# Attention feeding a two-layer MLP: one batch of tokens at a time, with attention steps woven between matmul groups in a written order

## The chip, the cores and the metric

The kernel runs on one core of a Trainium2 chip. A core has five engines with a queue each: TensorE (PE, matmuls out of SBUF into PSUM), VectorE (DVE), ScalarE (ACT), GpSimd (POOL, which here mostly issues DMAs) and SyncE (SP, which issues the output DMAs). Each queue runs its instructions in its own order, and instructions of different engines wait for one another by semaphores. PSUM has 8 banks of 512 fp32 values in each of 128 partitions. The metric is the device time of one execution in microseconds (us); lower is better.

## What is computed

Linear attention without softmax, an RMS norm per head, and a two-layer MLP with a PReLU, from the reference:

```python
batch, n_heads, seq, head_dim = (8, 8, 576, 64)
kv = np.einsum('bhsd,bhse->bhde', k, v)
out = np.einsum('bhsd,bhde->bhse', q, kv)
rms = np.sqrt(np.mean(out * out, axis=-1, keepdims=True) + 1e-06)
attn_out = (out / rms * g_norm)
x = attn_out.transpose(0, 2, 1, 3).reshape(B * S, H * D)      # 4608 x 512
h = x @ w_in                                                  # 512 x 2048
g = np.maximum(h, 0.0) + alpha * np.minimum(h, 0.0)
return (g @ w_out)                                            # 4608 x 512, fp32
```

## The kernel before

Data is fp32 in HBM; POOL's DMAs cast it to fp16 while loading. Heads are taken in pairs, so that one pair (2 x 64 rows) fills the 128 partitions: 4 pairs a batch, 32 in all.

Attention of a pair is split into four functions. `attn_fea` (L131 on) transposes q of the pair in five matmuls against an identity (L136, L145) and copies the result to SBUF on ACT. `attn_feb` makes k-transposed times v for each of the two heads in five matmuls of 64 columns (L163), copies it, and multiplies it with q-transposed for each head by itself, in a part of 512 and a part of 64 columns (L179, L183); DVE copies the result `ot` to SBUF. `attn_be1` squares it on DVE, sums the squares over the 64 rows of each head by a matmul with a two-column selector `esel` (L198, L201), and takes exp(-0.5 ln(mean + eps)) on two partitions on ACT (L205 to L214). `attn_be2` spreads the two rows back over 128 partitions by a matmul with `eselT` (L224, L227), and DVE multiplies `ot`, the gain and that into `xt` (L230, L235), which is kept for all 4608 tokens. `astep` (L288 on) runs these four functions for four different pairs in one call.

The MLP runs over 12 windows of 384 tokens. `moe_m1` makes the 16 blocks of 128 hidden features of a window, each from 4 chunks of the contraction (L247); ACT casts each block from PSUM to fp16 (L255) and DVE applies the PReLU as max(alpha h, h) (L257). `moe_m2` (L264 on) makes three tiles of 128 tokens, each from 16 matmuls of 512 columns (L269), copied by ACT (L277) and stored by SP.

The order of the work around it: for each window first as many `astep` calls as its tokens need, then the whole of `moe_m1` (64 matmuls in a row), two `astep` calls, the whole of `moe_m2` of the window before (48 in a row), two `astep` calls. All PSUM tiles share one pool of 8 banks. POOL loads q, k and v of batches 0 and 1, then w_in, w_out, then further batches, each batch as 3 tensors of 5 row chunks (L111). The identity is made behind the first of these loads.

Of the kernel before, what the change touches and what calls it, by code (L numbers as in the profile page):

```python
# [10 lines left out]
FP16 = mybir.dt.float16  # L12


@with_exitstack
def kernel(
# [11 lines left out]
    nc = tc.nc  # L28
# [7 lines left out]
    S_CH = [128, 128, 128, 128, 64]  # L36
    NT = len(S_CH)
    S_OFF = [0, 128, 256, 384, 512]
    NWIN = 384
    N_WINDOWS = N_TOK // NWIN  # L40
    NF = D_FF // P
    NC = D_MODEL // P
    assert NC == NPAIR
# [4 lines left out]
    xt_p = ctx.enter_context(tc.tile_pool(name="xt", bufs=1))  # L48
    qkv_p = ctx.enter_context(tc.tile_pool(name="qkv", bufs=3))
    attn_p = ctx.enter_context(tc.tile_pool(name="attn", bufs=2))  # L50
    gt_p = ctx.enter_context(tc.tile_pool(name="gt", bufs=2))
    ysb_p = ctx.enter_context(tc.tile_pool(name="ysb", bufs=3))
    psum_p = ctx.enter_context(tc.tile_pool(name="psum", bufs=8, space=bass.MemoryType.PSUM))
# [13 lines left out]
    ident = const_p.tile([P, P], FP32, name="ident")  # L67
# [8 lines left out]
    esel32 = const_p.tile([P, 2], FP32, name="esel32")  # L76
    nc.vector.memset(esel32[:], 0.0)
    nc.vector.memset(esel32[0:64, 0:1], 1.0)
    nc.vector.memset(esel32[64:128, 1:2], 1.0)
    esel = const_p.tile([P, 2], FP16, name="esel")  # L80
    nc.vector.tensor_copy(out=esel[:], in_=esel32[:])
    eselT_ps = psum_p.tile([2, P], FP32, name="eselT_ps", tag="pb")
    nc.tensor.matmul(
        out=eselT_ps[:], lhsT=esel32[:], rhs=ident[:, :], is_transpose=True,
        start=True, stop=True,
    )
    eselT = const_p.tile([2, P], FP16, name="eselT")
    nc.scalar.copy(out=eselT[:], in_=eselT_ps[:])

    g2col = const_p.tile([P, 1], FP32, name="g2col")  # L90
# [3 lines left out]
    alpha_sb = const_p.tile([P, NF], FP32, name="alpha_sb")  # L94
    with nc.allow_non_contiguous_dma("tiny alpha load"):
        nc.sync.dma_start(
            out=alpha_sb[:], in_=moe_alpha[:].rearrange("(g p) -> p g", p=P)
        )

    xt_sb = [xt_p.tile([P, N_TOK], FP16, name=f"xt{j}") for j in range(NC)]  # L100

    def load_qkv(b):
        tiles = {}
        for nm, src in (("q", q), ("k", k), ("v", v)):
            t = qkv_p.tile([P, NT, H, D], FP16, name=f"{nm}sb", tag=f"{nm}sb")
            tiles[nm] = t
            eng = nc.gpsimd
            for ti in range(NT):
                ps = S_CH[ti]
                st = S_OFF[ti]  # L110
                eng.dma_start(  # L111
                    out=t[0:ps, ti, :, :],
                    in_=src[b, :, st : st + ps, :].rearrange("h s d -> s h d"),
                )
        return tiles

    qkv0 = load_qkv(0)
    qkv1 = load_qkv(1)

    w_in_sb = []  # L120
    for c in range(NC):
        t = w_p.tile([P, D_FF], FP16, name=f"w_in_sb{c}")
        nc.gpsimd.dma_start(out=t[:], in_=moe_w_in[c * P : (c + 1) * P, :])
        w_in_sb.append(t)
    w_out_sb = []
    for g in range(NF):
        t = w_p.tile([P, D_MODEL], FP16, name=f"w_out_sb{g}")
        nc.gpsimd.dma_start(out=t[:], in_=moe_w_out[g * P : (g + 1) * P, :])  # L128
        w_out_sb.append(t)

    def attn_fea(b, j, tiles):  # L131
        qs = tiles["q"]
        hs = slice(2 * j, 2 * j + 2)
        qt_a = psum_p.tile([P, 512], FP16, name="qt_a", tag="pb")
        for ti in range(4):
            nc.tensor.matmul(  # L136
                out=qt_a[:, ti * 128 : (ti + 1) * 128],
                lhsT=qs[0:128, ti, hs, :],
                rhs=ident16[:, :],
                is_transpose=True,  # L140
                start=(ti == 0),
                stop=(ti == 3),
            )
        qt_b = psum_p.tile([P, 64], FP16, name="qt_b", tag="pb")
        nc.tensor.matmul(  # L145
            out=qt_b[:, 0:64], lhsT=qs[0:64, 4, hs, :], rhs=ident16[0:64, 0:64],
            is_transpose=True, start=True, stop=True,
        )
        qt_sb = attn_p.tile([P, S], FP16, name="qt_sb", bufs=3)
        nc.scalar.copy(out=qt_sb[:, 0:512], in_=qt_a[:])  # L150
        nc.scalar.copy(out=qt_sb[:, 512:576], in_=qt_b[:])
        return (b, j, tiles, qt_sb)

    def attn_feb(st):
        b, j, tiles, qt_sb = st
        ks, vs = tiles["k"], tiles["v"]
        hA = slice(2 * j, 2 * j + 1)
        hB = slice(2 * j + 1, 2 * j + 2)
        kv4 = psum_p.tile([P, 64], FP32, name="kv4", tag="pb")
        for half, hsel in ((0, hA), (1, hB)):  # L160
            for ti in range(NT):
                ps = S_CH[ti]
                nc.tensor.matmul(  # L163
                    out=kv4[64 * half : 64 * half + 64, :],
                    lhsT=ks[0:ps, ti, hsel, :],
                    rhs=vs[0:ps, ti, hsel, :],
                    start=(ti == 0),
                    stop=(ti == NT - 1),
                    tile_position=(0, 64 * half),
                )  # L170
        kv_sb = attn_p.tile([P, 64], FP16, name="kv_sb")
        nc.scalar.copy(out=kv_sb[:], in_=kv4[:])  # L172

        ot_a = psum_p.tile([P, 512], FP32, name="ot_a", tag="pb")
        ot_b = psum_p.tile([P, 64], FP32, name="ot_b", tag="pb")
        for half in range(2):
            rs = slice(64 * half, 64 * half + 64)
            tp = (64 * half, 64 * half)
            nc.tensor.matmul(  # L179
                out=ot_a[rs, :], lhsT=kv_sb[rs, :], rhs=qt_sb[rs, 0:512],  # L180
                start=True, stop=True, tile_position=tp,
            )
            nc.tensor.matmul(  # L183
                out=ot_b[rs, :], lhsT=kv_sb[rs, :], rhs=qt_sb[rs, 512:576],
                start=True, stop=True, tile_position=tp,
            )
        ot_sb = attn_p.tile([P, S], FP32, name="ot_sb", bufs=5)
        nc.vector.tensor_copy(out=ot_sb[:, 0:512], in_=ot_a[:])  # L188
        nc.vector.tensor_copy(out=ot_sb[:, 512:576], in_=ot_b[:])
        return (b, j, ot_sb)  # L190

    def attn_be1(st):
        b, j, ot_sb = st
        sq_sb = attn_p.tile([P, S], FP16, name="sq_sb")
# [25 lines left out]
    def attn_be2(st):  # L220
# [17 lines left out]
            op0=mybir.AluOpType.mult, op1=mybir.AluOpType.mult,  # L238
        )

    def moe_m1(w):
        n0 = w * NWIN
        gts = []
        for g in range(NF):
# [116 lines left out]
```

## Time and profile before

| | us |
|---|---|
| median of 3 runs | 399.4 |
| lowest and highest | 399.25, 403.49 |
| profiled execution: span from first to last instruction | 400.0 |
| PE busy in it | 361.5 (90%) |
| DVE, ACT, POOL busy in it | 194.1, 186.4, 111.9 |

The lines of the profile stand in the prediction, each ahead of what is read from it. "PE" rows are matmuls, "PEld" rows are weight loads. In a timeline row the columns are the start and the length of a run of equal instructions, engine, source line, operation, tiles (out<-in), shape and count, and in brackets the idle time in front with what ended it. In a row of the grouped lines the two numbers behind the first bar are the busy time in us and the mean length of one in ns; behind the second bar stands the engine's idle time ahead of them.

### The profile page before, as it was taken

How to read it: one execution, taken by the hardware profiler on the slowest of the kernel's cores; microseconds unless marked ns; L12 is line 12 of the kernel's file. 1: busy time of each engine (PE TensorE's matmuls, PEld its weight loads, DVE VectorE, ACT ScalarE, POOL GpSimd, SP SyncE). 2: the span in 40 equal slices, each digit the busy share in tenths (PEclk: the TensorE clock that was granted, in tenths of full speed). 3: DMA queues.
4: the chain of work that ended last, by engine and by line, in shares of the span. 5: the costliest groups of instructions: out<-in, count | busy, mean ns of one | idle time of the engine just before them, and what ended most of it. 6: DMA issues, size and time to landing. Idle time of an engine off the chain costs nothing.

```text
span 400.0 us, 5448 instructions
## 1 busy us (share of the span) xinstructions
PE 361.5 (90%) x2081; PEld 182.0 (45%) x2081; DVE 194.1 (49%) x358; ACT 186.4 (47%) x422; POOL 111.9 (28%) x146
## 2 busy tenths in 40 slices
PE   2389967999999999999999999979999999999996
PEld 0144433453445446344544534444545455555542
DVE  0056744594178149507825841780735444453600
ACT  2056644573367257426736733661535353444511
POOL 9992799998044440800000000000000000000000
PEclk9999985596989889698999969898999999999999
DMA  9999999999394963950001002001001010101022
GB/s 85 142 143 206 195 143 141 140 145 140 90 59 28 120 87 25 96 78 26 2 26 54 0 2 79 2 0 47 34 26 55 26 54 26 53 10 70 2 79 79
DMA packets 122826, 28.15 MB, mean 70 GB/s; under 512 B 115632, under 2 KB 117680, under 8 KB 122800
## 3 DMA queue, kind: packets, MB, share of 16 engines
q0 software_dynamic: 115392, 18.36, 62.1%
q1 hardware_dynamic: 7408, 9.45, 6.7%
q8 instruction: 16, 0.26, 0.3%
q14 instruction: 10, 0.08, 0.1%
HBM read 36.71 MB, written 9.44 MB: 115 GB/s over the span
## 4 chain that ended last, share of the span: by engine, by line
PE 74%; POOL 9%; ACT 8%; DMA 6%; issue 1%; DVE 1%; POOLq 0%; ACTq 0%
PE y_ps L269 34%; PE h_ps L247 31%; DMA w_in_sb<-in_moe_w_in_dram 3%; POOL vsb L111 3%; PE ot_a L179 3%; POOL qsb L111 3%; PE ssq_a L198 2%; POOL ksb L111 2%; ACT qt_sb L150 2%; ACT rstd L214 2%; DMA qsb<-in_q_dram 2%; PE rb_a L224 2%; ACT lnv L205 2%; PE kv L163 1%; DMA vsb<-in_v_dram 1%; POOL w_out_sb L128 1%
## 5 line engine op out<-in xcount | busy, mean ns | idle before, releaser
L257 DVE SCALAR_TENSOR_TENSOR gt<-h,alpha_sb 128x384 f16<-128x384 f16 x192 | 117.2, 618 | 54.3 <-ACT h L255 49.4
L269 PE MATMUL y_ps<-w_out_sb,gt 128*128 128x512 f16 x576 | 136.2, 400 | 0.0
L247 PE MATMUL h_ps<-xt,w_in_sb 128*128 128x384 f16 x768 | 134.9, 339 | 0.0
L255 ACT CAST h<-h_ps 128x384 f16<-128x384 f32 x192 | 91.1, 478 | 38.4 <-PE h_ps L247 37.1
L247 PEld LDWEIGHTS <-w_in_sb 128*128 128x128 f16 x768 | 77.1, 101 | 57.1 <-issue 11.0
L269 PEld LDWEIGHTS <-gt 128*128 128x128 f16 x576 | 58.3, 102 | 75.9 <-issue 15.6
L188 DVE COPY ot_sb<-ot_a 128x512 f32<-128x512 f32 x32 | 22.1, 691 | 110.1 <-PE ot_b L183 110.1
L277 ACT COPY y_sb<-y_ps 128x512 f32<-128x512 f32 x36 | 21.1, 586 | 111.7 <-PE y_ps L269 111.7
L111 POOL DMA_DIRECT2D qsb<-in_q_dram x40 | 34.3, 936 | 23.2 <-PE qt_b L145 22.7
L111 POOL DMA_DIRECT2D ksb<-in_k_dram x40 | 34.3, 961 | 23.1 <-PE kv L163 23.1
L163 PE MATMUL kv<-vsb,ksb 128*64 128x64 f16 (+1 forms) x320 | 31.2, 218 | 8.8 <-DMA vsb<-in_v_dram 8.8
L205 ACT ACTIVATE lnv<-ssq_a,eps_t 2x512 f32<-2x512 f32 x32 | 21.7, 677 | 33.1 <-PE ssq_b L201 33.1
L111 POOL DMA_DIRECT2D vsb<-in_v_dram x40 | 34.6, 994 | 0.5 <-DMA qsb<-in_q_dram 0.4
L230 DVE SCALAR_TENSOR_TENSOR xt<-ot_sb,g2col,rb_a 128x512 f16<-128x512 f32 x32 | 23.8, 743 | 15.8 <-PE rb_b L227 15.8
L163 PEld LDWEIGHTS <-ksb 128*64 128x64 f16 (+1 forms) x320 | 22.2, 120 | 15.9 <-issue 10.0
L179 PE MATMUL ot_a<-qt_sb,kv_sb 64*64 64x512 f16 x64 | 16.4, 504 | 12.8 <-ACT kv_sb L172 12.8
L150 ACT COPY qt_sb<-qt_a 128x512 f16<-128x512 f16 x32 | 18.5, 577 | 12.6 <-PE qt_a L136 12.6
L195 DVE TENSOR_TENSOR sq_sb<-ot_sb 128x576 f16<-128x576 f32 x32 | 24.0, 751 | 0.1
L136 PE MATMUL qt_a<-ident,qsb 128*128 128x128 f16 x128 | 15.9, 250 | 8.0 <-DMA qsb<-in_q_dram 8.0
L214 ACT ACTIVATE rstd<-lnv 2x576 f16<-2x576 f32 x32 | 21.7, 679 | 0.4
L136 PEld LDWEIGHTS <-qsb 128*128 128x128 f16 x128 | 9.6, 108 | 17.9 <-DMA qsb<-in_q_dram 9.4
L198 PE MATMUL ssq_a<-sq_sb,esel 128*2 128x512 f16 x32 | 15.0, 469 | 1.7 <-DVE sq_sb L195 1.7
(35 smaller groups left out, 118.2 us busy)
## 6 DMA issues: line engine op xcount, KB each, us to landing
out_dram<-y_sb SPq DMA_DIRECT2D x36, 256.0 KB, 2.0
qsb<-in_q_dram POOLq DMA_DIRECT2D x32, 128.0 KB, 4.6
ksb<-in_k_dram POOLq DMA_DIRECT2D x32, 128.0 KB, 4.6
vsb<-in_v_dram POOLq DMA_DIRECT2D x32, 128.0 KB, 4.6
w_in_sb<-in_moe_w_in_dram POOLq DMA_DIRECT2D x4, 512.0 KB, 10.3
w_out_sb<-in_moe_w_out_dram POOLq DMA_DIRECT2D x16, 128.0 KB, 4.9
qsb<-in_q_dram POOLq DMA_DIRECT2D x8, 64.0 KB, 4.3
ksb<-in_k_dram POOLq DMA_DIRECT2D x8, 64.0 KB, 4.5
```

What stands on the lines that cost most here:

```text
L111: eng.dma_start(out=t[0:ps, ti, :, :], in_=src[b, :, st : st + ps, :].rearrange("h s d -> s h d"),)
L136: nc.tensor.matmul(out=qt_a[:, ti * 128 : (ti + 1) * 128], lhsT=qs[0:128, ti, hs, :], rhs=ident16[:, :], is_transpose=True, start=(ti == 0 ...
L150: nc.scalar.copy(out=qt_sb[:, 0:512], in_=qt_a[:])
L163: nc.tensor.matmul(out=kv4[64 * half : 64 * half + 64, :], lhsT=ks[0:ps, ti, hsel, :], rhs=vs[0:ps, ti, hsel, :], start=(ti == 0), stop=(t ...
L179: nc.tensor.matmul(out=ot_a[rs, :], lhsT=kv_sb[rs, :], rhs=qt_sb[rs, 0:512], start=True, stop=True, tile_position=tp,)
L195: nc.vector.tensor_mul(out=sq_sb[:], in0=ot_sb[:], in1=ot_sb[:])
L205: nc.scalar.activation(out=lnv[:, 0:512], in_=ssq_a[:], func=mybir.ActivationFunctionType.Ln, bias=eps_t[0:2, :], scale=inv_d,)
L214: nc.scalar.activation(out=rstd2[:], in_=lnv[:], func=mybir.ActivationFunctionType.Exp, bias=0.0, scale=-0.5,)
L247: nc.tensor.matmul(out=h_ps[:], lhsT=w_in_sb[c][:, g * P : (g + 1) * P], rhs=xt_sb[c][:, n0 : n0 + NWIN], start=(c == 0), stop=(c == NC - 1),)
L255: nc.scalar.copy(out=h16[:], in_=h_ps[:])
L257: nc.vector.scalar_tensor_tensor(out=gt[:], in0=h16[:], scalar=alpha_sb[:, g : g + 1], in1=h16[:], op0=mybir.AluOpType.mult, op1=mybir.Alu ...
L269: nc.tensor.matmul(out=y_ps[:], lhsT=gts[g][:, a * P : (a + 1) * P], rhs=w_out_sb[g][:], start=(g == 0), stop=(g == NF - 1),)
```

## The change

The kernel is rewritten around one batch (576 tokens) at a time:

- The tokens of a batch are two halves of 288 columns. Every PSUM tile of attention's `ot` and norm sum and of the first layer's block is two banks, one half in each, and one instruction of ACT or DVE takes both halves (576 values).
- A pair's k-transposed times v is made as one 128 x 128 product in five matmuls, and the blocks off the diagonal are set to zero by a multiplication with a mask on DVE. `ot` then takes two matmuls for both heads.
- The squares are summed by a matmul with the same mask in fp16 (128 x 128 blocks of ones), so that the sum stands on all 128 partitions at once. The selector, its transposition and the spreading matmuls are gone; Ln and Exp run on 128 partitions.
- The PReLU is h + (1 - alpha) relu(-h): a Relu on ACT out of PSUM, then one DVE instruction that reads PSUM too.
- PSUM is split by use: two tiles of two banks for the first layer, one bank for the second, one bank for q-transposed and kv (`ps_s`), one tile of two banks for `ot` and the norm sum (`ps_b`).
- The order of all engines is the order of the program text. A stream of steps (ot, t, ssq, kv of neighbouring pairs, 16 steps a batch) is taken one step at a time behind each of the 16 first-layer groups, with a share of the second-layer matmuls between them.
- Batch 0 is loaded in halves of 4 heads, ahead of the identity; w_in and w_out come in four pieces each, and w_in comes ahead of batch 1.

The diff, cut to its core (what is taken away stands whole in the listing above):

```diff
+    ps_h = ctx.enter_context(tc.tile_pool(name="psh", bufs=2, space=bass.MemoryType.PSUM))
+    ps_y = ctx.enter_context(tc.tile_pool(name="psy", bufs=1, space=bass.MemoryType.PSUM))
+    ps_s = ctx.enter_context(tc.tile_pool(name="pss", bufs=1, space=bass.MemoryType.PSUM))
+    ps_b = ctx.enter_context(tc.tile_pool(name="psb", bufs=1, space=bass.MemoryType.PSUM))
+    ctx.enter_context(tc.manual_schedule(engines={ENG.PE, ENG.Activation, ENG.DVE, ENG.Pool, ENG.SP}))
...
+    for j in range(0, NPAIR, 2):
+        for nm in ("k", "v", "q"):
+            load_heads(0, nm, 2 * j, 2 * j + 4)
...
+    load_w_in()
+    load_batch(1)
+    load_w_out()
+    load_batch(2)
...
+    def step_t(st):
...
+        st["qt"] = attn_p.tile([P, S], FP16, name="qt_sb")
+        nc.vector.tensor_copy(out=st["qt"][:], in_=qt_ps[:, 0:S])
+    def step_kv(st):
...
+        nc.vector.tensor_mul(out=st["kv"][:], in0=kv_ps[:], in1=mask32[:])
+    def step_ot(st):
+        ot_ps = ps_b.tile([P, 2, 512], FP32, name="ot_ps", tag="b")
+        for i in range(2):
+            nc.tensor.matmul(
+                out=ot_ps[:, i, 0:HS], lhsT=st["kv"][:], rhs=st["qt"][:, i * HS : (i + 1) * HS],
+                start=True, stop=True,
+            )
...
+        nc.scalar.activation(out=st["sq"][:], in_=ot_ps[:, :, 0:HS], func=AF.Square)
...
+        nc.vector.tensor_copy(out=st["ot"][:], in_=ot_ps[:, :, 0:HS])
+    def step_ssq(st):
...
+                out=ssq_ps[:, i, 0:HS], lhsT=mask16[:], rhs=st["sq"][:, i, :],
...
+            out=lnv[:], in_=ssq_ps[:, :, 0:HS], func=AF.Ln, bias=eps_t[:], scale=inv_d,
...
+        nc.scalar.activation(out=rstd[:], in_=lnv[:], func=AF.Exp, bias=0.0, scale=-0.5)
+        nc.vector.scalar_tensor_tensor(
+            out=xts[b, j][:],
+            in0=st["ot"][:], scalar=g2col[:], in1=rstd[:], op0=ALU.mult, op1=ALU.mult,
+        )
+    def step_stream():
+        for b in range(B):
+            st = [{"b": b, "j": j} for j in range(NPAIR)]
+            for j in range(NPAIR + 1):
+                if j > 0:
+                    yield step_ot, st[j - 1], False
+                if j < NPAIR:
+                    yield step_t, st[j], False
+                if j > 0:
+                    yield step_ssq, st[j - 1], j == NPAIR
+                if j < NPAIR:
+                    yield step_kv, st[j], False
...
+    def m1_group(b, g, big=False):
+        pool, tag = (ps_b, "b") if big else (ps_h, "h")
+        h_ps = pool.tile([P, 2, 512], FP32, name="h_ps", tag=tag)
+        for c in range(NC):
+            for i in range(2):
+                nc.tensor.matmul(
+                    out=h_ps[:, i, 0:HS], lhsT=w_in_blk(c, g), rhs=xts[b, c][:, i, :],
+                    start=(c == 0), stop=(c == NC - 1),
                 )
...
+        nc.scalar.activation(out=m_sb[:], in_=h_ps[:, :, 0:HS], func=AF.Relu, scale=-1.0)
...
+            in0=m_sb[:], scalar=beta_sb[:, g : g + 1], in1=h_ps[:, :, 0:HS],
...
+    class M2:
...
+        def run(self, n, limit):
+            while n > 0 and self.t < limit:
+                if self.g == 0:
+                    self.y = ps_y.tile([P, 512], FP32, name="y_ps", tag="y")
+                y_mm(self.y[:], self.t, self.g)
+                self.g += 1
+                n -= 1
+                if self.g == NF:
+                    y_out(self.y[:], self.t)
+                    self.t, self.g = self.t + 1, 0
...
+    attn_until(0)
     for g in range(NF):
+        m1_group(0, g, g % 3 == 2)
+    ya = ps_h.tile([P, 2, 512], FP32, name="ya", tag="h")
+    yb = ps_h.tile([P, 2, 512], FP32, name="yb", tag="h")
+    ys = [ya[:, 0, :], ya[:, 1, :], yb[:, 0, :], yb[:, 1, :]]
+    for g in range(NF):
+        for t in range(4):
+            y_mm(ys[t], t, g)
+        attn_step()
+    for t in range(4):
+        y_out(ys[t], t)
+    m2.t = 4
+    attn_until(1)
+    for b in range(1, B):
+        if b + 2 < B:
+            load_batch(b + 2)
+        limit = (b * S) // P
+        total = max(0, (limit - m2.t) * NF - m2.g)
+        done = 0
         for g in range(NF):
+            m1_group(b, g)
+            want = total * (g + 1) // NF
+            m2.run(want - done, limit)
+            done = want
+            attn_step()
...
+    m2.run(10**9, N_TOK // P)
```

By this text batch 1 has no second-layer matmuls between its groups (`limit` is 4, and those tiles are done), batches 2, 4 and 6 have 80 (5 behind each group), batches 3, 5 and 7 have 64 (4 behind each group), and the last 80 stand behind everything.

Three places show what moves. On POOL at the start, before (loads are q, k, v of batch 0; `ident` is the identity):

```order
masks.py:197 MEMSET ident 128x128
L111 DMA qsb<-in_q_dram 128x8x64
masks.py:199 ISA
masks.py:199 AFFINE_SELECT ident<-ident 128x128
L111 DMA qsb<-in_q_dram 128x8x64 x3
L111 DMA qsb<-in_q_dram 64x8x64
```

On POOL at the start, now:

```order
L89 DMA vsb_93<-in_v_dram 128x4x64 x4
L89 DMA vsb_93<-in_v_dram 64x4x64
L89 DMA qsb_95<-in_q_dram 128x4x64 x4
L89 DMA qsb_95<-in_q_dram 64x4x64
masks.py:197 MEMSET ident 128x128
masks.py:199 ISA
masks.py:199 AFFINE_SELECT ident<-ident 128x128
L133 DMA w_in_sb_159<-in_moe_w_in_dram 128x4x512
```

The identity, on which the transposes of q wait, moved from behind one load to behind all thirty of batch 0, which are half as large each.

On DVE in the attention of batch 0, before (`ot_sb` is the copy of `ot`, `sq_sb` the squares):

```order
L230 SCALAR_TENSOR_TENSOR xt_104<-ot_sb,g2col,rb_a 128x512 [waits DMAHW1_49,DMAHW0_49,PE_49]
L235 SCALAR_TENSOR_TENSOR xt_104<-ot_sb,g2col,rb_b 128x64 [waits PE_49]
L195 TENSOR_TENSOR sq_sb<-ot_sb 128x576 [waits DVE_49]
L188 COPY ot_sb<-ot_a 128x512 [waits PE_49]
L189 COPY ot_sb<-ot_b 128x64 [waits PE_49]
```

On DVE at the same place, now (`kv_sb` is the masked kv):

```order
L216 COPY ot_sb<-ot_ps 128x576 [waits Activation_49]
L189 COPY qt_sb<-qt_ps 128x576 [waits PE_49]
L233 SCALAR_TENSOR_TENSOR xt<-ot_sb,g2col,rstd 128x576 [waits DVE_49,Activation_49]
L204 TENSOR_TENSOR kv_sb<-kv_ps,mask_153 128x128 [waits PE_49]
L216 COPY ot_sb<-ot_ps 128x576 [waits Activation_49]
```

The copies of kv and of q-transposed came over from ACT, the squares went there, the copy of `ot` waits for ACT's Square, and the kv of a pair stands behind the `xt` of the pair before, which waits for ACT's Exp.

On PE where a second-layer tile ends and the next begins, before (weights `gt` are the hidden values of 128 tokens):

```order
L269 MATMUL y_ps<-w_out_sb_180,gt 128x512
L269 LDWEIGHTS gt
L269 MATMUL y_ps<-w_out_sb_182,gt 128x512
L269 LDWEIGHTS gt
L269 MATMUL y_ps<-w_out_sb_152,gt 128x512 [waits PE_49]
```

On PE at such a place now, inside the work of batch 2 (one of the four per batch that fall inside a run):

```order
L296 MATMUL y_ps<-w_out_sb_188,gt 128x512
L296 LDWEIGHTS gt
L296 MATMUL y_ps<-w_out_sb_182,gt 128x512 [waits Activation_49]
L296 LDWEIGHTS gt
L296 MATMUL y_ps<-w_out_sb_182,gt 128x512
L196 LDWEIGHTS ksb_91
L196 MATMUL kv_ps<-vsb_93,ksb_91 128x128 [waits DVE_49]
```

With one bank for the second layer, the first matmul of a tile waits for ACT's copy of the tile before; the attention step and the next first-layer group stand behind it on PE.

More of the change, by code (lines that the diff above doesn't have):

```diff
@@ L91 @@
-    nc.sync.dma_start(out=g2col[0:64, :], in_=g_norm[:].unsqueeze(1))
-    nc.sync.dma_start(out=g2col[64:128, :], in_=g_norm[:].unsqueeze(1))
[L94 to L97, printed above, removed]
-        )
[L100 to L113, printed above, removed]
-                )
-        return tiles
@@ L117 @@
[L117 to L125, printed above, removed]
-    for g in range(NF):
[L127 to L190, printed above, removed]
```

305 lines of the change are left out of this document (153 added, 152 removed).

## The prediction

> **What bounds the kernel now.** I read the page first: busy shares, the slices of time, and the shares of the chain that ended last.
>
> ```profile
> span 400.0 us, 5448 instructions
> PE 361.5 (90%) x2081; PEld 182.0 (45%) x2081; DVE 194.1 (49%) x358; ACT 186.4 (47%) x422; POOL 111.9 (28%) x146
> PEclk9999985596989889698999969898999999999999
> PE 74%; POOL 9%; ACT 8%; DMA 6%; issue 1%; DVE 1%; POOLq 0%; ACTq 0%
> ```
>
> TensorE (PE) is the bound, no other engine is half busy, and the granted clock dips until about 270 us. Next the chain in order of time, for where PE is not the bound and for the pure price of a matmul.
>
> ```profile
> 26.85 1.36 POOL w_in_sb L123 x3
> 28.21 13.20 DMA w_in_sb<-in_moe_w_in_dram
> ...
> 302.88 10.40 PE h_ps L247 x64
> 313.28 10.36 PE y_ps L269 x48
> ...
> 375.56 20.73 PE y_ps L269 x96
> 396.30 0.03 ACTq L277
> ...
> 396.36 0.58 ACT y_sb L277
> ```
>
> Until 41 us the chain is POOL issuing loads, then the w_in transfer. At the end PE runs without a gap: 10.40/64 = 162.5 ns for 384 columns, 10.36/48 = 215.8 ns for 512. Last PE's timeline, one attention burst of two pairs and what follows such bursts.
>
> ```profile
> 183.90 12.25 PE L247 MATMUL h_ps<-xt,w_in_sb 128*128 128x384 f16 x64
> 195.99 0.39 PE L136 MATMUL qt_a<-ident,qsb 128*128 128x128 f16 x4
> 196.31 0.20 PE L145 MATMUL qt_b<-ident,qsb 64*128 64x64 f16 x1
> 196.44 0.84 PE L163 MATMUL kv<-vsb,ksb 128*64 128x64 f16 x10
> 197.58 0.41 PE L179 MATMUL ot_a<-qt_sb,kv_sb 64*64 64x512 f16 x2 [0.30 <-ACT kv_sb L172]
> ...
> 198.63 0.40 PE L136 MATMUL qt_a<-ident,qsb 128*128 128x128 f16 x4
> ...
> 200.54 0.41 PE L179 MATMUL ot_a<-qt_sb,kv_sb 64*64 64x512 f16 x2 [0.60 <-ACT kv_sb L172]
> ...
> 201.59 10.53 PE L269 MATMUL y_ps<-w_out_sb,gt 128*128 128x512 f16 x48
> ```
>
> A pair costs 198.63 - 195.99 = 2.64 us. After the burst before 183.90 the 64 h matmuls took 12.25 instead of 10.4 us; after the burst at 195.99 nothing was lost. So a burst sits at the edge of what the clock bears, and a drop costs about 1.7 us.
>
> **PE prices of the change.** From 384 to 512 columns a matmul grows by 53.3/128 = 0.416 ns a column, so 288 columns cost 162.5 - 96 x 0.416 = 122.5 ns. Bounds: transposes of 128 columns are 80 ns apart ((196.31 - 195.99)/4), more than that line gives, so weight loads show at narrow shapes; a line from 80 to 162.5 ns gives 131.6 ns at 288. The 1024 first-layer matmuls cost 125.4 us, at most 134.7, against 768 x 162.5 = 124.8 now. I take 122.5, since 288 is nearer 384 and lies above the 80 ns floor. The 576 second-layer matmuls stay at 124.3 us. A pair becomes 5 transposes x 80, 5 kv matmuls x 84 (the ten now take 0.84), 2 + 2 x 122.5 ns = 1.31 us. The 1.33 us saved (rb gone, kv halved, the two ot halves in one) make 42.6 us over 32 pairs. PE's work is then 125.4 + 124.3 + 41.9 = 292 us; the rest of the sum is waits.
>
> **Evacuation prices.**
>
> ```profile
> L230 DVE SCALAR_TENSOR_TENSOR xt<-ot_sb,g2col,rb_a 128x512 f16<-128x512 f32 x32 | 23.8, 743 | 15.8 <-PE rb_b L227 15.8
> L235 DVE SCALAR_TENSOR_TENSOR xt<-ot_sb,g2col,rb_b 128x64 f16<-128x64 f32 x32 | 8.8, 275 | 0.0
> L188 DVE COPY ot_sb<-ot_a 128x512 f32<-128x512 f32 x32 | 22.1, 691 | 110.1 <-PE ot_b L183 110.1
> L189 DVE COPY ot_sb<-ot_b 128x64 f32<-128x64 f32 x32 | 6.8, 214 | 0.0
> L205 ACT ACTIVATE lnv<-ssq_a,eps_t 2x512 f32<-2x512 f32 x32 | 21.7, 677 | 33.1 <-PE ssq_b L201 33.1
> L209 ACT ACTIVATE lnv<-ssq_b,eps_t 2x64 f32<-2x64 f32 x32 | 9.2, 288 | 0.0
> L214 ACT ACTIVATE rstd<-lnv 2x576 f16<-2x576 f32 x32 | 21.7, 679 | 0.4
> L172 ACT CAST kv_sb<-kv 128x64 f16<-128x64 f32 x32 | 6.6, 206 | 12.2 <-PE kv L163 12.0
> L255 ACT CAST h<-h_ps 128x384 f16<-128x384 f32 x192 | 91.1, 478 | 38.4 <-PE h_ps L247 37.1 <-DVE gt L257 0.8
> L277 ACT COPY y_sb<-y_ps 128x512 f32<-128x512 f32 x36 | 21.1, 586 | 111.7 <-PE y_ps L269 111.7
> L269 PE MATMUL y_ps<-w_out_sb,gt 128*128 128x512 f16 x576 | 136.2, 400 | 0.0
> ```
>
> Stretched to 576 elements by the slope between the long and short row: DVE's gate or xt 0.81 us, a copy 0.76 (taken for the f16 one too), the mask product of 128 about 0.34; ACT's Ln 0.73, Exp 0.68, Relu or Square 0.67 (between 0.64, the line of L255 and L277, and 0.68). A wait on PE adds the drain, 400 - 216 = 0.18 us, and a handover 0.05 (the 0.30 before ot_a holds the 0.206 copy of L172 and two of them). Per step of the new loop ACT has about 1.35 us (a Relu, a quarter of Square, Ln, Exp, some y copies) and DVE 1.45 (a gate and a quarter of 2.67), PE 2.2: neither becomes the bound, except where the second layer is missing (batch 1).
>
> **The sum by stages** (each line ends with the time since the span's start at which the stage is over). Start: all 30 loads of batch 0, at half size, now stand ahead of the identity that the transposes need.
>
> ```profile
> 2.37 0.31 POOL masks.py:199 TENSOR_SCALAR_AFFINE_SELECT ident<-ident 128x128 f32<-128x128 f32 x1
> 5.90 4.23 POOL L111 DMA_DIRECT2D ksb<-in_k_dram  x5
> 10.04 4.27 POOL L111 DMA_DIRECT2D vsb<-in_v_dram  x5
> L111 POOL DMA_DIRECT2D ksb<-in_k_dram x5: 766/931/945, 5.9 to 9.4; - x5
> DMA to landing us min/median/max: 4.3/4.5/4.8
> L128 POOL DMA_DIRECT2D w_out_sb<-in_moe_w_out_dram x16 | 8.7, 577 | 10.0 <-DMA w_in_sb<-in_moe_w_in_dram 9.0 <-issue 0.3
> 35.06 1.15 PE L163 MATMUL kv<-vsb,ksb 128*64 128x64 f16 x10
> ...
> 39.00 1.15 PE L163 MATMUL kv<-vsb,ksb 128*64 128x64 f16 x10
> 42.23 11.46 PE L247 MATMUL h_ps<-xt,w_in_sb 128*128 128x384 f16 x64
> ```
>
> Four full loads take (9.4 - 5.9)/4 = 0.875 us each, the fifth with half the runs 0.64. So 24 x 0.64 + 6 x 0.52 = 18.5 us (bounds 12.5, if cost goes by bytes, and 24.8, if halving saves nothing); transposes start at 20.5. Batch 0 has no other work beside it. On DVE each mask product stands behind the xt of the pair before, so the cycle of a pair at half clock is ot 0.64, Square 0.67, ot copy 0.76 (it waits for the Square), norm sum 0.64, Ln 0.73, Exp 0.68, xt 0.81, mask 0.34 and eight handovers: 5.7 us, where it is 3.9 now (kv at 35.06 and 39.00 in the same stretch). First ot at 23.3, last xt at 45.6. No transfer is late. A load waits for the landing of the load eight before it, 8 x 0.62 = 5.0 us of issuing against 4.5 to land. POOL is done with batch 0 at 19.5, w_in takes 13.2 us as now: 35. Behind it 15 loads of batch 1 (12.5 us of issuing, and about the 9.0 that POOL waits now for w_in) put w_out's issue at 44 and, at w_in's 13.2 us for the same bytes, its landing at 57; it is first needed at 62.6.
> First layer of batch 0: 16 x 0.98 + 1.3 until the clock is up (11.46 against 10.40 now): to 62.6.
> First four y tiles with attention of batch 1: 64 x 0.216 + 5.2, 1.2 until the last gate frees yb, and per pair 1.0 of the chain Ln, Exp, xt, mask, ot (3.1 us, covered by 2.1): to 86.8.
> Batch 1, without second-layer work: 2.9 at entry (Ln, Exp and two y copies before a PSUM buffer is free; a gap like this probably costs one clock drop, 1.7), then four pairs of 5.2 + 1.8 stall, the chain being longer by Relus and gates between: to 119.4.
> Batches 2, 4, 6: 15.7 + 80 x 0.216 + 5.2 = 38.2. Five y matmuls stand in each step, so four of five y tiles end inside a run, and with one y bank the next matmul waits for Relu 0.67 and y copy 0.59: 1.4 + 1.2 + 1.4 (behind Ln and Exp) + 0.9 = 4.9. Entry: drain, Ln, Exp, xt and handovers 2.6, less the six matmuls of the other three chunks 0.73 = 1.85. Together 45.0 each.
> Batches 3 and 5: four y matmuls a step, so tiles end between runs, under the next attention step and first-layer group (1.25 us against 0.9): 34.7 + 1.85 = 36.6 each. Batch 7, no attention: 29.5 + 1.85 = 31.4. To 359.0.
> Tail: 80 x 0.216 + 5 x 0.9 (drain, copy, two handovers, nothing beside them) = 21.8, then 3.7 as now (396.3 to 400.0): 384.5 of span. The profiled span of 400.0 stands 0.6 over the median of 399.4, so 384 us.
>
> Nothing is charged for DVE's nine memsets and the masks (under POOL's issuing), the output DMAs (four y buffers) or later loads, each issued a batch or more ahead.
>
> **A rule against it.** In this trace PE has no gap after 302 us and the clock holds, so frequent short gaps in dense work are not shown. The Trainium skill (TensorE: Matmul & The Clock Gate, "A second HAM failure mode: psum-queue depth-cycling") says that PE idling briefly between groups as it cycles PSUM buffers made the clock swing between half and full. By that rule the sum would be the first rival's.
>
> **Rivals.** (1) The clock drops at the new gaps. Where the walk has 7 entries, 12 y stalls, 4 waits in batch 1 and 5 in the tail, each drop costs 1.7 us: half of them make 384 + 14 x 1.7 = 408, slower, and 12 decide it (403.4). For it: bursts with 0.30 and 0.60 us of idle lose the clock. Against: those bursts are made of small tiles, the burst at 195.99 kept it, and a 1.85 us gap here lies between full-size matmuls. (2) Waits are covered better than walked (shorter prologue, chains overlapped, most y and entry stalls gone): 28 of the 48 us of waits that the walk has behind the start (384.5 - 45.6 - 286.8 of PE work - 3.7) are hidden, which gives 356. For it: ACT and DVE have slack. Against: one y bank makes the order strict. (3) Weight loads show at 288 columns: 384 + 9.3 = 393; the 80 ns row is for it, no exposure at 384 against. (4) Halving loads saves nothing on POOL: 384 + 6.3 = 390.
>
> **How the numbers follow.** Forecast 0.58 (372 to 396 by its own bounds), clock 0.13, covered waits 0.17, weight loads 0.06, POOL 0.06. The time is the forecast's, 384. The range 364 to 400 leaves out most of the clock case and the lowest part of the second. A measurement here can tell about 1%: faster is under 395.4, slower over 403.4. Forecast (0.55 of 0.58), rivals 2, 4 and nothing of 3 make 0.78 faster; 3, the top of the forecast and a few drops make 0.12 the same; the clock beyond 12 drops 0.10 slower.
>
> **What would show it.** First transposes near 20.5 us, first h matmul of the last chunk near 46; h matmuls 122 ns apart; PE waits on the y copy of about 1 us in batches 2, 4, 6 and the tail and none in 3 and 5; a wait of 1.8 us on xt at each entry; clock 1.0 after about 125 us. A clock at 0.9 there, or spacing near 130 ns, would break the sum; so would PE waiting for a transfer.

## The result, and the profile after

The changed kernel takes 378.6 us (median of 4 runs, 378.05 to 379.55), beside 401.2 us for the kernel before on the same chip (399.25 to 403.49): a ratio of 0.943, 95% interval 0.937 to 0.949. The forecast was 384 us, in a range of 364 to 400.

The page of the profile, first its shares and the granted clock:

```profile
span 376.4 us, 5119 instructions
PE 300.3 (80%) x2049; PEld 191.0 (51%) x2049; DVE 175.1 (47%) x272; ACT 167.9 (45%) x261; POOL 116.4 (31%) x149
PEclk9999999998999999999999999999999999999999
```

PE is busy 61 us less than before and waits more: 76 us of the span against 38.5. The clock line dips in one slice only. It doesn't show the start, though: five transposes take 0.69 us at 24.67 and 0.44 us at 122.51 (both rows stand below), and the line reads 9 at both places. Behind the start, PE went from a throttled engine with few gaps (22 us of idle time behind 44 us, at a clock of 0.91 from 120 to 270 us) to a full-speed engine with more of them (39 us behind 48.5 us). PE's waits by what ended them (total, how often, the longest):

```profile
PE alpha_ps L162 <- POOL ident masks.py:199: 23.6, 1, 23.6
PE y_ps L296 <- ACT y_sb L303: 13.6, 17, 1.0
PE ot_ps L209 <- DVE kv_sb L204: 12.2, 11, 2.1
PE h_ps L276 <- DVE xt L233: 12.1, 7, 1.9
PE ssq_ps L222 <- DVE ot_sb L216: 5.7, 6, 1.5
PE h_ps L276 <- ACT y_sb L303: 2.5, 1, 2.5
```

For the y bank and the entries the numbers are those of the forecast: 17 for the y bank (12 inside batches 2, 4 and 6, five in the tail), and an entry for each of batches 2 to 7 (the seventh wait for xt is 0.96 us in batch 0; batch 1's entry is the single 2.5 us). None is for a transfer. PE's timeline at the places the forecast named:

```profile
24.67 0.69 PE L180 MATMUL qt_ps<-ident,qsb 128*128 128x128 f16 x5 [0.82 <-DVE beta_sb L168]
...
26.98 0.66 PE L209 MATMUL ot_ps<-qt_sb,kv_sb 128*128 128x288 f16 x2 [0.38 <-DVE kv_sb L204]
...
32.41 0.66 PE L209 MATMUL ot_ps<-qt_sb,kv_sb 128*128 128x288 f16 x2 [2.07 <-DVE kv_sb L204]
...
48.50 17.53 PE L276 MATMUL h_ps<-xt,w_in_sb 128*128 128x288 f16 x122 [0.96 <-DVE xt L233]
65.87 0.59 PE L296 MATMUL ya<-w_out_sb,gt 128*128 128x512 f16 x2
...
88.09 0.41 PE L222 MATMUL ssq_ps<-sq_sb,mask 128*128 128x288 f16 x2 [0.67 <-DVE ot_sb L216]
91.00 2.08 PE L276 MATMUL h_ps<-xt,w_in_sb 128*128 128x288 f16 x8 [2.51 <-ACT y_sb L303]
...
118.63 0.90 PE L276 MATMUL h_ps<-xt,w_in_sb 128*128 128x288 f16 x6
121.19 0.41 PE L276 MATMUL h_ps<-xt,w_in_sb 128*128 128x288 f16 x2 [1.66 <-DVE xt L233]
...
122.51 0.44 PE L180 MATMUL qt_ps<-ident,qsb 128*128 128x128 f16 x5
122.79 1.14 PE L276 MATMUL h_ps<-xt,w_in_sb 128*128 128x288 f16 x8
123.77 1.24 PE L296 MATMUL y_ps<-w_out_sb,gt 128*128 128x512 f16 x5
124.85 0.44 PE L196 MATMUL kv_ps<-vsb,ksb 128*128 128x128 f16 x5
125.13 1.14 PE L276 MATMUL h_ps<-xt,w_in_sb 128*128 128x288 f16 x8
...
129.79 1.02 PE L296 MATMUL y_ps<-w_out_sb,gt 128*128 128x512 f16 x4 [1.00 <-ACT y_sb L303]
...
161.62 0.90 PE L276 MATMUL h_ps<-xt,w_in_sb 128*128 128x288 f16 x6
164.43 0.40 PE L276 MATMUL h_ps<-xt,w_in_sb 128*128 128x288 f16 x2 [1.91 <-DVE xt L233]
```

Starts are to be subtracted, since a row runs past the start of the next (122.79 + 1.14 is beyond 123.77). 123.77 - 122.79 = 0.98 for eight first-layer matmuls is 122.5 ns each; 122.79 - 122.51 = 0.28 for the five transposes of a step is 56 ns each, and so is 125.13 - 124.85 for the five of kv; batch 2 runs from 118.63 to 161.62, 43.0 us. By stages, forecast and measured:

| stage | forecast us | measured us |
|---|---|---|
| start, to the first h matmul of the last chunk | 46 | 48.5 |
| first layer of batch 0 ends | 62.6 | 65.9 |
| four y tiles with attention of batch 1 | 24.2 | 22.4 |
| batch 1 | 32.6 | 30.3 |
| batches 2, 4, 6 | 45.0 each | 43.0 to 43.2 |
| batches 3, 5 | 36.6 each | 35.75 |
| span | 384.5 | 376.4 |

### The profile page after: what moved, and what is told of

Read it like the earlier page. It is cut to its first block, busy times and chain, and to the rows that moved or that the text cites. A ratio compares the mean times of both kernels' runs of the same rounds, so it can differ in the third digit from the quotient of the medians.

```text
span 376.4 us, 5119 instructions
## 1 busy us (share of the span) xinstructions
PE 300.3 (80%) x2049; PEld 191.0 (51%) x2049; DVE 175.1 (47%) x272; ACT 167.9 (45%) x261; POOL 116.4 (31%) x149
## 4 chain that ended last, share of the span: by engine, by line
PE 71%; ACT 13%; DVE 7%; POOL 6%; issue 3%; ACTq 0%; POOLq 0%
PE h_ps L276 30%; PE y_ps L296 29%; ACT y_sb L303 4%; ACT lnv L227 4%; DVE xt L233 3%; ACT rstd L232 3%; PE ot_ps L209 3%; PE qt_ps L180 2%; PE ssq_ps L222 2%; POOL ksb L89 2%; POOL vsb L89 2%; POOL qsb L89 2%; PE kv_ps L196 2%; DVE ot_sb L216 1%; ACT m_sb L286 1%
## 5 line engine op out<-in xcount | busy, mean ns | idle before, releaser
L276 PE MATMUL h_ps<-xt,w_in_sb 128*128 128x288 f16 x1024 | 149.6, 292 | 14.9 <-DVE xt L233 12.1
L287 DVE SCALAR_TENSOR_TENSOR gt<-m_sb,beta_sb,h_ps 128x576 f16<-128x576 f32 x128 | 104.0, 813 | 78.1 <-ACT m_sb L286 77.9
L286 ACT ACTIVATE m_sb<-h_ps 128x576 f32<-128x576 f32 x128 | 83.0, 648 | 103.5 <-PE h_ps L276 103.5
L276 PEld LDWEIGHTS <-w_in_sb 128*128 128x128 f16 x1024 | 100.2, 100 | 45.0 <-issue 17.1
L233 DVE SCALAR_TENSOR_TENSOR xt<-ot_sb,g2col,rstd 128x576 f16<-128x576 f32 x32 | 26.2, 819 | 46.4 <-ACT rstd L232 46.4
L214 ACT ACTIVATE sq_sb<-ot_ps 128x576 f16<-128x576 f32 x32 | 20.8, 651 | 55.9 <-PE ot_ps L209 55.9
L216 DVE COPY ot_sb<-ot_ps 128x576 f32<-128x576 f32 x32 | 24.2, 758 | 23.6 <-ACT sq_sb L214 23.6
L227 ACT ACTIVATE lnv<-ssq_ps,eps_t 128x576 f32<-128x576 f32 x32 | 23.7, 742 | 21.4 <-PE ssq_ps L222 21.4
L209 PE MATMUL ot_ps<-qt_sb,kv_sb 128*128 128x288 f16 x64 | 14.2, 306 | 12.2 <-DVE kv_sb L204 12.2
L232 ACT ACTIVATE rstd<-lnv 128x576 f32<-128x576 f32 x32 | 21.8, 682 | 1.0
L180 PE MATMUL qt_ps<-ident,qsb 128*128 128x128 f16 x160 | 15.6, 233 | 0.8 <-DVE beta_sb L168 0.8
```

What stands on the lines that cost most here:

```text
L180: nc.tensor.matmul(out=qt_ps[:, t * P : (t + 1) * P], lhsT=qs[:, t, 2 * j : 2 * j + 2, :], rhs=ident16[:], is_transpose=True, start=(t == ...
L209: nc.tensor.matmul(out=ot_ps[:, i, 0:HS], lhsT=st["kv"][:], rhs=st["qt"][:, i * HS : (i + 1) * HS], start=True, stop=True,)
L216: nc.vector.tensor_copy(out=st["ot"][:], in_=ot_ps[:, :, 0:HS])
L227: nc.scalar.activation(out=lnv[:], in_=ssq_ps[:, :, 0:HS], func=AF.Ln, bias=eps_t[:], scale=inv_d,)
L232: nc.scalar.activation(out=rstd[:], in_=lnv[:], func=AF.Exp, bias=0.0, scale=-0.5)
L233: nc.vector.scalar_tensor_tensor(out=xts[b, j][:], in0=st["ot"][:], scalar=g2col[:], in1=rstd[:], op0=ALU.mult, op1=ALU.mult,)
```

## The experiments

Two questions stood open: which part of the change made the gain (cheaper pairs, or the woven order with its full clock), and whether the waits above are worth what the walk through them says. All ratios are to the kernel before, run on the same chip (medians 400 to 403 us).

**Arithmetic alone.** The kernel before with its windows, its order and its pool of PSUM banks, and only a pair's arithmetic from the change:

```diff
-                    out=kv4[64 * half : 64 * half + 64, :],
...
+                out=kv4[:], lhsT=ks[0:ps, ti, hs, :], rhs=vs[0:ps, ti, hs, :],
...
+        nc.vector.tensor_mul(out=kv_sb[:], in0=kv4[:], in1=mask32[:])
...
+            out=ot_a[:], lhsT=kv_sb[:], rhs=qt_sb[:, 0:512], start=True, stop=True
...
-            out=ssq_a[:], lhsT=esel[:], rhs=sq_sb[:, 0:512], start=True, stop=True
+            out=ssq_a[:], lhsT=mask16[:], rhs=sq_sb[:, 0:512], start=True, stop=True
...
-            out=rb_a[:], lhsT=eselT[:], rhs=rstd2[:, 0:512], start=True, stop=True
```

> The kernel before, in its own order and with its own windows and PSUM pool, with only the new arithmetic of a pair: masked kv in five matmuls of 128 columns, ot in one product for both heads, norm sum by the 128x128 mask, Ln and Exp on 128 partitions, no rb. Theory 1 (the cheaper pair on PE is most of the gain, and the woven order mainly pays for its own waits): about 1.2 us less per pair where PE is the bound, 24 to 32 pairs, and shorter bursts that hold the clock better: 360 to 375 us. Theory 2 (the gain is the weaving, which keeps the clock up and hides the chains): the bursts stay bound by their chains and keep losing the clock, 385 to 395 us.

Measured: 364.8 us (364.27 to 367.61), ratio 0.913 (0.906 to 0.921). That is 14 us faster than the whole change: the arithmetic alone is worth more than all of it, and the rest of the change gives some back. PE's timeline around a burst of two pairs of this kernel:

```profile
113.81 0.39 PE L129 MATMUL qt_a<-ident,qsb 128*128 128x128 f16 x4
114.13 0.20 PE L138 MATMUL qt_b<-ident,qsb 64*128 64x64 f16 x1
114.26 0.56 PE L154 MATMUL kv<-vsb,ksb 128*128 128x128 f16 x5
...
115.90 0.39 PE L129 MATMUL qt_a<-ident,qsb 128*128 128x128 f16 x4
...
118.21 10.52 PE L238 MATMUL y_ps<-w_out_sb,gt 128*128 128x512 f16 x48
```

A pair costs 2.1 us where it cost 2.64, and the burst of 4.4 us (it was 5.6) is followed by matmuls at full speed.

**Spreading alone.** The kernel before with its own arithmetic and one pair at a time where it had two in a row:

```diff
+            if g % 8 == 7:
+                astep()
...
+            if a != 1 and w < N_WINDOWS - 1:
+                astep()
...
-        astep()
-        astep()
...
-        astep()
-        astep()
+        else:
+            astep()
+            astep()
```

> The kernel before, arithmetic and buffers unchanged, with its attention calls taken one at a time (in the middle and at the end of a window's first layer, behind the first and the third y tile) instead of two in a row. Theory A (a burst of two pairs is long enough to lose the clock, one pair is not): the matmul groups that took 11.5 to 13.0 us return to 10.4, up to 20 us less in all: 379 to 385 us. Theory B (the clock goes by the share of small matmuls, however placed): as before, 398 to 402.

Measured: 379.6 us (378.7 to 382.0), ratio 0.948 (0.941 to 0.954). The same stretch in the kernel before and in this one; the columns are length, busy us and count of PE, PEld, DVE, ACT and POOL, then the granted clock. Before:

```profile
120.00:270.00 150.00, 140.71 (x868) 70.94 (x867) 85.33 (x160) 79.53 (x187) 20.96 (x25) 0.91 0.37 42
```

One pair at a time:

```profile
120.00:270.00 150.00, 145.17 (x947) 76.18 (x946) 89.75 (x172) 85.91 (x198) 19.73 (x24) 1.00 0.38 47
```

The clock goes from 0.91 to 1.00 and PE gets through 947 matmuls instead of 868. No work was removed. Between the two profiled executions (spans of 400.0 and 380.2 us) PE is busy 17.0 us less, 344.5 against 361.5, and idle 2.8 us less. So most of the gain is throttling behind bursts that single pairs of 2.6 us don't cause. Not all of the throttling goes: from 44 to 120 us, where PE waits for the loads of batch 1, the clock is 0.84 here and 0.80 before.

**Both.** The two edits together:

> The kernel before with the new arithmetic of a pair and one pair at a time between matmul groups instead of two in a row. Alone the arithmetic gave 364.8 and the spreading 379.6, from 400. Theory: both take away the same loss, the throttled matmuls behind a burst of two pairs; with the cheaper pair the burst is already short enough for the full clock, so spreading adds nothing: 362 to 367. Rival: they are separate gains and the 20 us of the spreading come again: 343 to 348.

Measured: 359.5 us (358.98 to 360.7), ratio 0.894 (0.889 to 0.899). Neither number was met: spreading added 5 us, far from 20 but not nothing. Where they lie shows in the stretches in which batch 1's loads come in. Arithmetic alone:

```profile
38.00:60.00 22.00, 17.34 (x85) 8.56 (x83) 14.62 (x25) 11.16 (x24) 17.12 (x25) 0.91 1.65 175
60.00:75.00 15.00, 10.99 (x48) 5.09 (x49) 8.33 (x17) 7.36 (x18) 15.00 (x20) 0.50 2.23 143
```

Both:

```profile
38.00:60.00 22.00, 12.25 (x52) 5.39 (x51) 9.08 (x17) 6.99 (x15) 16.67 (x24) 0.82 1.62 175
60.00:75.00 15.00, 13.15 (x88) 7.39 (x87) 12.92 (x26) 11.46 (x28) 15.00 (x19) 0.92 2.20 141
```

From 38 to 60 us the kernel with both edits is behind (52 matmuls against 85), from 60 to 75 us ahead (88 against 48): with the arithmetic alone PE meets four pairs in a row there, waits for v in them and runs at half clock. Behind 110 us the two kernels are alike, with 1355 and 1352 matmuls up to 357 us, both at a clock of 1.00. So the 5 us lie ahead of 110 us, and behind it the two edits take away the same throttling, as the theory had it.

**Un-weaving.** The changed kernel with the 16 attention steps of a batch taken eight at a time:

```diff
-            attn_step()
+            if g % 8 == 7:
+                for _ in range(8):
+                    attn_step()
```

> The changed kernel with its attention steps of batches 2 to 7 taken eight at a time behind every eighth first-layer group instead of one behind each. Theory 1 (walk of the prediction): a pair alone takes about 5 us on its chain through ACT and DVE against 1.3 of PE work, so about 3.5 us more for each of 24 pairs, 85 us, and the clock drops in each of 12 bursts, 1.7 to 3.4 us each: 470 to 500 us. Rival (the chain is mostly overlapped by engines working ahead, so the weaving is worth little): under 400 us.

Measured: 490.1 us (one run), 22% over the kernel before's 400.3. Its clock and its longest waits:

```profile
PEclk9999999887769798697958979588976979869999
...
PE ot_ps L209 <- DVE kv_sb L204: 51.6, 31, 2.6
PE ssq_ps L222 <- DVE ot_sb L216: 29.1, 23, 1.5
```

So the change needs matmuls between its attention steps. Against the changed kernel PE idles 65 us more, nearly all of it in these two waits, and at a mean clock of 0.87 it is busy 47 us longer. The longer wait is for data: ot needs the masked kv, which DVE makes behind the xt of the pair before. The other is for the one big tile, which the norm sum gets only when ot is copied out. How much of this comes from the split of PSUM, and how much from the order of the steps, is not shown: no run changes the banks alone.

**The y waits.** The changed kernel with the second-layer matmuls of batches 2, 4 and 6 dealt out so that a tile ends where a run ends (3, 3, 3, 3 and 4 steps a tile instead of 5 matmuls a step):

```diff
             want = total * (g + 1) // NF
+            if total == 5 * NF:
+                steps = [3, 6, 9, 12, 16]
+                k = next(i for i, e in enumerate(steps) if g < e)
+                lo = steps[k - 1] if k else 0
+                want = NF * k + NF * (g + 1 - lo) // (steps[k] - lo)
```

> The changed kernel with the y matmuls of batches 2, 4 and 6 dealt out so that each y tile ends at the end of a run (3, 3, 3, 3 and 4 steps a tile). The four mid-run waits a batch on the y copy, 1.00, 0.78, 0.93 and 0.67 us in batch 2, should go: 12 waits, 10.1 us, so 368 to 370 us against 378.6. Rival (ACT or DVE paces the woven loop, so that the wait moves to the next buffer): 376 to 379.

Measured: 366.1 us (365.87 to 366.5), ratio 0.915 (0.910 to 0.920), 12.5 us faster than the change. PE's wait for the y copy:

```profile
PE y_ps L296 <- ACT y_sb L303: 3.4, 5, 0.7
```

Only the five of the tail are left. The 12 others held 10.2 us, and each also stood behind the last matmul's drain. The miss in the expectation is 2 us to the good.

**The identity.** The changed kernel with `make_identity` ahead of the loads of batch 0:

```diff
+    ident = const_p.tile([P, P], FP32, name="ident")
+    make_identity(nc, ident[:])
+
     srcs = {"q": q, "k": k, "v": v}
...
-    ident = const_p.tile([P, P], FP32, name="ident")
-    make_identity(nc, ident[:])
```

> The changed kernel with the identity made ahead of the loads of batch 0, as in the kernel before. The first transposes then wait for q of the first four heads (issued by 12.8 us, landing 3.3 later), at 16 instead of 24.7 us: 8.5 us less, 370 us. Rival (weights or later batches arrive too late and take the gain back): first h matmul earlier, but a new wait on w_out or on q of batch 2, and 374 to 378.

Measured: 369.6 us (368.67 to 369.81), ratio 0.923 (0.918 to 0.928): 9.0 us. First transposes and the first h matmul of the last chunk:

```profile
11.54 0.29 PE L181 MATMUL qt_ps<-ident,qsb 128*128 128x128 f16 x1 [8.75 <-DMA qsb<-in_q_dram]
...
39.41 2.80 PE L277 MATMUL h_ps<-xt,w_in_sb 128*128 128x288 f16 x11 [0.96 <-DVE xt L234]
```

The transposes start 13 us earlier, but the second half of q lands only at 23 to 25 us, so 9.1 of the 13 arrive (48.50 to 39.41).

**Whole loads.** The identity left behind the loads, and batch 0 in 15 whole loads instead of 30 half ones (`load_batch(0)` in place of the loop over `load_heads`):

> The changed kernel with batch 0 loaded in 15 whole loads instead of 30 halves; the identity stays behind them. Theory (POOL pays 0.72 us per half load against 0.83 per whole one, so halving nearly doubles the issuing): identity at 14.5 us instead of 23.5, q of the last rows lands at 18, first transposes at 18.3 instead of 24.7: 6 us less, 372 to 373 us. Rival (the bytes set the pace, not the number of loads): no change.

Measured: 370.6 us (370.07 to 371.69), ratio 0.925 (0.919 to 0.930): 8.1 us, by another way to the same wait. POOL's timeline of this kernel:

```profile
1.25 4.33 POOL L89 DMA_DIRECT2D ksb<-in_k_dram  x5 [0.80 <-POOLq L370]
5.53 4.24 POOL L89 DMA_DIRECT2D vsb<-in_v_dram  x5
9.67 4.28 POOL L89 DMA_DIRECT2D qsb<-in_q_dram  x5
13.80 0.35 POOL masks.py:197 MEMSET ident<- 128x128 f32 x1
```

The identity is begun at 13.8 us. Both edits together were not tried.

**The entry.** The first run of y matmuls of a batch ahead of its first group, so that they lie in the wait for xt:

```diff
-            m1_group(b, g)
+            if g > 0:
+                m1_group(b, g)
...
             done = want
+            if g == 0:
+                m1_group(b, g)
```

> The changed kernel with the first run of y matmuls of each batch ahead of its first first-layer group. Theory (entry waits on xt, 1.7 to 1.9 us each, are a lack of other work at that place): the four or five y matmuls fill 0.9 to 1.1 us of six entries, but the first of them now waits about 0.4 for the y copy: 4 to 7 us less, 372 to 375 us. Rival (ACT's queue is what is late there, and y copies ahead of Ln make xt later by as much): no change, 377 to 380.

Measured: 372.1 us (371.73 to 372.65), ratio 0.928 (0.923 to 0.934): 6.5 us. The two waits that answer to it:

```profile
PE y_ps L296 <- ACT y_sb L303: 15.7, 22, 1.0
...
PE h_ps L276 <- DVE xt L233: 3.4, 7, 1.0
```

8.7 us of entry waits go and 2.1 come back as five more waits for the y bank.

**kv earlier.** Step kv ahead of step ssq, so that a pair's mask product doesn't stand behind the xt of the pair before on DVE:

> The changed kernel with step kv taken ahead of step ssq in the stream, so that on DVE the mask product of a pair no longer stands behind the xt of the pair before. Theory (that place in DVE's queue makes the waits of PE for kv_sb, 12.2 us in all): the three waits of 0.60 in the y stage and of 1.14 in batch 1 go, and batch 0's cycle shrinks by 0.4 to 0.8 a pair: 5 to 8 us less, 371 to 374 us against 378.6. Rival (the chain through ssq and its one PSUM buffer is as long): under 2 us.

Measured: 376.4 us (376.31 to 378.49), ratio 0.941 (0.933 to 0.948): 2.2 us, where 5 to 8 were expected. This was a miss. PE's waits of that kernel:

```profile
PE kv_ps L196 <- DVE qt_sb L189: 7.0, 9, 1.4
PE ssq_ps L222 <- DVE ot_sb L216: 4.1, 3, 1.6
...
PE ot_ps L209 <- ACT lnv L227: 2.5, 3, 0.8
```

Of the 12.2 us for kv_sb 0.4 are left, but q-transposed and kv share one bank, so kv now waits for the copy of qt, and ot waits for Ln to free the big tile. The wait moved to the next single buffer.

**The waits together.** The y waits, the identity and the entry in one kernel, and then the same with kv earlier:

> The changed kernel with three edits that were each run alone: tiles of batches 2, 4 and 6 end at run ends, identity ahead of the loads, first run of y matmuls ahead of the first group of a batch. Theory: each takes away a different wait of TensorE (y_ps on y_sb inside the run; the transposes' start; h_ps on xt at a batch's entry), nothing else of the kernel is near its limit, so the gains add: 378.6 - 12.5 - 9.0 - 6.5 = 350.6, taken as 349 to 352. Rival: with these waits gone the next ones show (loads of a batch, the copy of y, the steps' own single buffers), and a third or more of the sum is given back: 358 or more.

> The same three edits and step kv ahead of step ssq as a fourth. Alone that edit gave 2.2 us, because the wait for kv_sb turned into waits for the copies of qt and for Ln. Theory: the same 2 us come again, 347 to 350. Rival: with the earlier start the pairs of batch 0 stand behind the copy of qt, and the fourth edit gives nothing or loses beside the three: 350 to 354.

Measured: 350.9 us (350.76 to 351.56), ratio 0.873 (0.867 to 0.878), against a sum of 350.6; with the fourth edit 349.5 us (349.33 to 349.83), ratio 0.869 (0.865 to 0.874). PE's line in the page of the first:

```profile
PE 300.2 (86%) x2049; PEld 190.5 (55%) x2049; DVE 175.0 (50%) x272; ACT 168.3 (48%) x261; POOL 116.4 (33%) x149
```

PE's busy time is the change's 300.3 us less 0.1; only waits went. They beat the change by 28 and 29 us, and the best version in the order of the kernel before (359.5) by 9 and 10. That the woven order is the better one doesn't follow from this. The kernel of 359.5 us takes the fifth chunk of q, k and v with 64 rows, where the change pads it to 128, and in the changed kernel the padding alone is worth 8.9 us (next experiment). The order of the kernel before with the padding was not run.

**The fifth chunk.** One forecast price was off: a pair costs PE less than the walk has. The changed kernel with the fifth chunk of q, k and v as its 64 rows instead of 128 with zeros:

```diff
-                out=qt_ps[:, t * P : (t + 1) * P],
-                lhsT=qs[:, t, 2 * j : 2 * j + 2, :],
-                rhs=ident16[:],
+                out=qt_ps[:, t * P : t * P + n],
+                lhsT=qs[0:n, t, 2 * j : 2 * j + 2, :],
+                rhs=ident16[0:n, 0:n],
...
-                lhsT=ks[:, t, 2 * j : 2 * j + 2, :],
-                rhs=vs[:, t, 2 * j : 2 * j + 2, :],
+                lhsT=ks[0:n, t, 2 * j : 2 * j + 2, :],
+                rhs=vs[0:n, t, 2 * j : 2 * j + 2, :],
```

> The changed kernel with the fifth chunk of q, k and v taken as 64 rows in the transposes and the kv product, where the change takes it as 128 rows whose lower half is zero. The prediction charged 80 ns for a transpose and 84 for a kv matmul, read off bursts whose fifth instruction had 64 rows; in the changed kernel five of either take 0.28 us, 56 ns each. Theory: the 80 was no price of the 128-row ones but the step to the 64-row one, so the two steps of a pair grow from 0.28 to about 0.40 us each where matmuls stand behind them: 28 pairs x 0.25 = 7, 384 to 388. Rival: the rows of the chunk don't matter, and the 56 ns come from where the steps stand in the stream: 378 to 380.

Measured: 387.5 us (386.47 to 389.14), ratio 0.965 (0.958 to 0.971): 8.9 us slower than the change. The same rows as in the changed kernel's timeline above:

```profile
122.60 0.52 PE L181 MATMUL qt_ps<-ident,qsb 128*128 128x128 f16 x5
123.05 1.15 PE L278 MATMUL h_ps<-xt,w_in_sb 128*128 128x288 f16 x8
...
125.12 0.55 PE L198 MATMUL kv_ps<-vsb,ksb 128*128 128x128 f16 x5
125.60 1.16 PE L278 MATMUL h_ps<-xt,w_in_sb 128*128 128x288 f16 x8
```

The steps take 0.45 and 0.48 us instead of 0.28 each, 0.37 us more a pair. Fewer rows, in the transposes fewer columns too, and longer. Where the time goes shows in the rows of the arithmetic alone, whose fifth chunk has 64 rows as well. Four transposes 56 ns apart would bring the fifth 0.22 us behind the first; it starts 0.32 us behind it (114.13 - 113.81; its row says 64*128), and the next matmul another 0.13 us later. So both the step to the 64-row instruction and the step away from it are long, and the four others are not.

## Why the prediction was right, and where it wasn't

The forecast's mechanism held: PE stays the bound, the clock stays up, and what is left is a count of waits, whose main places were right one by one. It ended 5.4 us high in the time and 8.1 us high in the span, as a sum of terms with both signs: the start and the first layer 3.3 short, everything behind them 11.4 long. Part of the closeness is luck: the two partly cancel, and so does the last step, from span to time. The forecast took the time as 0.6 us less than the span, from the span of one execution and the median of several; the changed kernel's profiled execution took 378.55 us at a span of 376.4, 2.2 us more.

- *PE prices.* 122.5 ns for 288 columns came out exactly, so no weight load shows there. The pair was the term that was mis-sized. The 80 ns of a transpose is the step from four of 128 rows to one of 64, spread over the four; the 84 ns of a kv matmul is the mean of ten, two of which have 64 rows. The extra time belongs to the 64-row ones, not to the others. A pair costs 0.28 + 0.28 + 2 x 0.245 = 1.05 us instead of 1.31, and 28 pairs lie between matmuls: about 7.3 of the 11.4 us. With the 64-row chunk put back, a pair costs 1.42. The forecast was for an instruction that the change had removed; the diff's zero-padded chunk showed it.
- *The y waits.* The four of batch 2 last 1.00, 0.78, 0.93 and 0.67 us, with their drains about 4.0 instead of 4.9; three batches make 2.7 us of the 11.4. Which of the summed latencies is too long was not looked into. Taking the 12 away gave 12.5 us, about these waits and their drains (12.1).
- *Entry, tail, batch 1.* Entries 1.66 to 1.91 us against 1.85; in the tail a tile's wait and drain make about 0.85, against 0.9. The gap at batch 1's entry, 2.51 us behind one of 0.67, did cost a clock drop (its first two groups are 2.40 and 1.91 us apart, the later ones 1.26: 1.8 us, charged at 1.7). The stalls were over-charged: without the price of the pairs, the y stage is 0.8 us and batch 1 1.3 us shorter than forecast. With the two items above this makes 12.0 us, of which other places took 0.6 back.
- *The start.* The loads are mis-sized: 0.62 us was charged a half load, and it takes 0.71. POOL's timeline of the changed kernel:

```profile
1.25 3.75 POOL L89 DMA_DIRECT2D ksb<-in_k_dram  x5 [0.80 <-POOLq L372]
4.95 3.64 POOL L89 DMA_DIRECT2D vsb<-in_v_dram  x5
...
22.69 0.46 POOL masks.py:197 MEMSET ident<- 128x128 f32 x1
```

  (22.69 - 1.25)/30 = 0.71, 2.9 us over the forecast, and another 1.2 us for the alpha transposition and the identity's copies ahead of the first transposes, which weren't charged. The pair's cycle at half clock, 5.43 us against 5.7, gives some of it back.
- *The rivals.* Beyond the one at batch 1's entry, the clock's drops didn't come: 17 gaps of 0.67 to 1.0 us and six of 1.66 to 1.91 us between full-size matmuls left the mean granted clock at 0.995. The Trainium skill (TensorE: Matmul & The Clock Gate, "A second HAM failure mode: psum-queue depth-cycling") tells of a kernel in which brief idle times between groups of matmuls made the clock swing; this trace doesn't agree. Weight loads at 288 columns didn't show. Halved loads saving little on POOL was nearly half right (2.9 of its 6.3 us). Covered waits were true by about 5 of the 28 us: 2.7 in the y waits and 2.1 in the stalls of the y stage and batch 1.

The forecast got the time nearly right without asking what each part was worth. The arithmetic alone gives 35.5 us (400.3 to 364.8), and the rest of the change, the padded chunk's gain included, gives 14 of them back. That rest's cost lies in the waits that the forecast charged: the 12 y waits, the identity and the entries are 28 us, shown by taking them away singly (12.5, 9.0 and 6.5) and together (27.7). The prediction counted them as the price of the order; they were not, since each went with a few lines.

## What to carry to other kernels

Price an instruction from rows of one shape only: where a row's neighbour has another shape, the step between them is in the difference of their starts. When the bound engine is throttled, look at how long the bursts of small work ahead of the slow stretches are; breaking bursts of 5.6 us into halves was worth 20 us here, against 23 for the rewrite. Waits of a hand-set order that the trace puts at different places add up, and can be taken away one by one; a wait between steps that share one buffer only moves to the next of them.

## What the runs showed of the hardware

- A matmul of 64 rows among 128-row ones makes the five of a step longer, not shorter: 0.28 us becomes 0.45 for the transposes and 0.48 for kv. Padding the chunk with zeros is the cheaper form by 0.37 us a pair. The time lies in the step to the 64-row instruction and in the step away from it; why is not settled here.
- Issuing a load on POOL goes neither by bytes nor by count: five half loads take 3.54 to 3.70 us (0.71 to 0.74 each), five whole ones 4.13 to 4.28.
- Gaps of up to 1.91 us between full-size matmuls leave the granted clock at 1.00 here; one of 2.51 us, two matmuls behind one of 0.67, is followed by 2.4 us at 0.51. Bursts of two pairs of small matmuls with idle gaps of 0.3 to 0.6 us often lose the clock when they last 5.6 us (mean 0.91 from 120 to 270 us), and keep it at 1.00 when they last 4.4 us (arithmetic alone, behind 110 us) or, with one pair, 2.6 us (spreading alone, from 120 to 270 us).
